# Every fourth plain-product PSUM tile moves from a pool of six banks to a pool of two

## The chip, the cores and the metric

The kernel runs on one core of one Trainium2 chip. The metric is the device time of one execution in microseconds (us); the time of a kernel is the median of several executions. A core has a matrix engine (TensorE, PE in the profile), a vector engine (VectorE, DVE), an activation engine (ScalarE, ACT), GpSimd (POOL) and SyncE (SP), which here only issues transfers (DMA). TensorE writes its products into PSUM, which this program uses as eight banks of 128 x 512 fp32; VectorE and ScalarE read them out. Weight loads of TensorE have their own row, PEld.

## The reference

With x of 2048 rows and 1024 columns, all inputs bf16, the reference computes two branches and mixes them by a gate per row:

```
g  = sigmoid((x * gate_w).sum(-1))
a  = attention(x @ wqkv) @ wo            # 32 heads of 32; each row sees 8 keys, 2 rows apart, backwards
z  = gelu(x @ w_in)                      # 3584 columns
z1 = z[:, :1792];  z2 = layernorm(z[:, 1792:])
b  = (z1 * (w_sp @ z2 + b_sp)) @ w_out   # w_sp is 2048 x 2048
out = g * a + (1 - g) * b
```

## The kernel before

The program is written out flat, and each engine runs its instructions in the order in which they were written. Some work is placed by a planner (class `Beat`, L237): it keeps a clock that advances with the columns that TensorE has been given (`beat.run`), and emits small jobs (loads, norms, pieces of the attention on VectorE) when they are due by that clock.

TensorE's work comes in stages. First come the products for z2 and for q, k, v, interleaved: `z2_block` (L307, matmuls on L312) and `qkv_tile` (L602, matmuls on L607), 64 and 128 tiles. Then comes the z1 stage (L700 to L718): 64 tiles, numbered 0 to 63 below, each of 8 matmuls of 448 columns (L710), evacuated by ScalarE with a gelu (L712) into one of two staging slots of four tiles, `z1s_slots`, which SP stores to DRAM after every fourth tile (L717). Then comes the mixing stage: 16 groups (`g_group`, L752) of seven products of 8 matmuls each (L725), a Strassen-like scheme for w_sp @ z2. Then comes the product with wo (L877 to L886, 32 tiles `psa`), and the last stage (L900 to L935), eight blocks of seven products with w_out. z1, the mixing and the last stage need VectorE to prepare sums of operands (`s_sums`, L487; `t_sums`, L496; `y_sums`, `w_sums`), and VectorE also does the whole attention between the z2 stage and the end of the mixing.

PSUM is divided in two pools (L82, L83): `psum` with six banks and `seeded` with two. Within a pool a tile takes the bank that has been free longest; its first matmul waits until the bank's last reader is done. Before the change the plain products (z2, qkv, z1, wo) and the `pa`, `pd` tiles of the mixing and last stage all take banks of `psum`. The banks of `seeded` serve the warm-up (L105) and `fork` (L744): there ScalarE copies a half-done sum from a `psum` bank into a `seeded` bank, and TensorE goes on adding to that copy.

Three other jobs lie inside the z1 stage. `row_store` (L465), due 20 us after its beginning by the planner's clock, takes a `psum` bank `pt` for two small transposes (L467, L468), which VectorE reads with two small instructions (L469, L470) that stand in VectorE's queue behind attention and layernorm work; the store to `rs_d` that follows (L474) waits for VectorE, and the stores and loads issued after it wait behind it on SP. `squares` (L668, L671) and `w_norm` (L542, L543) are ScalarE passes over 1792 columns each, ten and eight of them in this stage; `w_norm` reads pieces of w_out that SP loads into two slots (L540). `w_power` (L550) takes one more `psum` bank before the last four tiles, read by VectorE (L553).

In a group of the mixing, `fork` (L749), `keep` (L735, L737), the copy of `pb` (L767) and the last piece (L776) are ScalarE's; two additions (L741) and the product with z1 (L777) are VectorE's. `scale_rows` (L485) and `s_sums` (L489, L490) for the next pair of groups stand in VectorE's queue after the first group of the pair before.

Of the kernel before, what the change touches and what calls it, by code (L numbers as in the profile page):

```python
# [10 lines left out]
F32 = mybir.dt.float32  # L11
# [4 lines left out]
P = 128  # L16
# [40 lines left out]
def _sub_ap(t, offset_elems, dims):  # L57
    return bass.AP(tensor=t.tensor, offset=t.offset + offset_elems, ap=[list(t.ap[0])] + [list(d) for d in dims])
# [3 lines left out]
def kernel(  # L62
# [19 lines left out]
    psum = ctx.enter_context(tc.tile_pool(name="psum", bufs=6, space=bass.MemoryType.PSUM))  # L82
    seeded = ctx.enter_context(tc.tile_pool(name="seeded", bufs=2, space=bass.MemoryType.PSUM))  # L83
# [4 lines left out]
    def reg(off, n):  # L88
        return arena[:, off:off + n]
# [6 lines left out]
    rs_d = dpool.tile([S], BF, name="rs_d")  # L96
    wop_d = dpool.tile([D, D], BF, name="wop_d")
    o_d = dpool.tile([S, D], BF, name="o_d")

    warm = reg(R_OFF + 35200, 512)  # L100
    nc.vector.memset(warm, 0.0)
# [180 lines left out]
    def v_order(g):  # L282
        wgt = wg_slots[g % 3]
        vdst = wgt[:, 2, :, :].rearrange("p k (d h) -> p k d h", d=DH, h=HG)
        vsrc = wgt[:, 3, :, :].rearrange("p k (h d) -> p k d h", h=HG, d=DH)
        nc.scalar.copy(vdst, vsrc)
# [17 lines left out]
    def z2_tile(i, c):  # L304
        z2_block([(i, c)])

    def z2_block(blocks):  # L307
        banks = [psum.tile([P, 512], F32, name="ps", tag="ps") for _ in blocks]
        for kt in range(KT):
            for ps, (i, c) in zip(banks, blocks):  # L310
                N = ZC + 1 if c == 3 else ZC
                nc.tensor.matmul(ps[:, 0:N], xT[:, kt, i * P:(i + 1) * P], w2[:, kt, ZC * c:ZC * c + N],  # L312
                                 start=(kt == 0), stop=(kt == KT - 1))
        for ps, (i, c) in zip(banks, blocks):
            z2_out(ps, i, c)

    def z2_out(ps, i, c):
        nc.scalar.activation(z2[:, i, ZC * c:ZC * (c + 1)], ps[:, 0:ZC], ACT.Gelu_apprx_tanh,  # L318
                             accum_out=s1[:, 4 * i + c:4 * i + c + 1])
        if c == 3:  # L320
            nc.scalar.copy(gl_s[:, i:i + 1], ps[:, ZC:ZC + 1])
        beat.run(KT * ZC)
# [199 lines left out]
    def load_w1(c):  # L522
        sync.dma_start(w1_slots[c], win_v[:, :, ZC * c:ZC * (c + 1)])
# [32 lines left out]
    def load_rows_y(u):  # L556
        for r in range(2):
            sync.dma_start_transpose(rows[u % 5].whole[r], y_d[(2 * u + r) * P:(2 * u + r + 1) * P, :])
# [42 lines left out]

    def qkv_tile(g, j):  # L602
        wgt = wg_slots[g % 3]
        ps = psum.tile([P, 512], F32, name="ps", tag="ps")
        for kt in range(KT):
            lhsT = xT[:, kt, j * P:(j + 1) * P] if g == 0 else _sub_ap(xT_flat, kt * S + j, [[NJ, P]])
            nc.tensor.matmul(ps[:, 0:3 * C].rearrange("p (t c) -> p t c", t=3), lhsT, wgt[:, 0:3, kt, :],  # L607
                             start=(kt == 0), stop=(kt == KT - 1))
        st = stage_slots[stg[0] % 3]
        if g == 0:  # L610
            nc.scalar.copy(st[:, j % 4, 0:2 * C], ps[:, 0:2 * C])
            nc.scalar.copy(st[:, j % 4, 2 * C:3 * C].rearrange("p (d h) -> p d h", h=HG),
                           ps[:, 2 * C:3 * C].rearrange("p (h d) -> p d h", h=HG))
        else:
            nc.scalar.copy(st[:, j % 4, :], ps[:, 0:3 * C])  # L615
        if j % 4 == 3:
            row, step, first = (C, P * C, (j - 3) * P) if g == 0 else (NJ * C, C, j - 3)
            for n, (t_d, off) in enumerate(((q_d, g * S), (k_d, g * (S + 16) + 16), (v_d, g * (S + 16) + 16))):
                sync.dma_start(bass.AP(tensor=t_d.tensor, offset=t_d.offset + (off + first) * C,
                                       ap=[[row, P], [step, 4], [1, C]]), st[:, :, n * C:(n + 1) * C])  # L620
            stg[0] += 1
        if j == 8 and g + 1 < NG:
            v_order(g + 1)
        projected[g] += 1
        beat.run(KT * 3 * C)

    warm_up(6)
    xpose(0, 2)
    z2_block([(i, c) for c in range(2) for i in range(2)])
    for i in range(2, 8):  # L630
        z2_tile(i, 0)
    beat.steps = vector_steps(beat.now + NJ * KT * 3 * C * BEAT + 8.0)
    for j in range(NJ):
        qkv_tile(0, j)
# [11 lines left out]
    for g in range(1, NG):  # L646
        if g + 1 < NG:
            load_wg(g + 1)
        for j in range(NJ):
            qkv_tile(g, j)  # L650
        if g == 1:
            for i in range(8, 16):
                z2_tile(i, 0)
# [14 lines left out]
    def squares():  # L668
        i = square[0]
        square[0] += 1  # L670
        nc.scalar.activation(junk[:, 0:FH], z2[:, i, :], ACT.Square, accum_out=s2[:, i:i + 1])  # L671
        if i % 4 == 3:
            beat.at(beat.now + 4.0, lambda i=i: stats(i))
            for ii in range(i - 3, i + 1):
                beat.at(beat.now + 8.0, lambda ii=ii: norm(ii))
# [24 lines left out]
    for c in range(4):  # L700
        w1 = w1_slots[c]
        if c == 0:
            load_w1(2)
        for i in range(16):
            if c == 2 and i == 6:
                load_w1(3)
            z1s = z1s_slots[(i // 4) % 2]
            ps = psum.tile([P, 512], F32, name="ps", tag="ps")
            for kt in range(KT):
                nc.tensor.matmul(ps[:, 0:ZC], xT[:, kt, i * P:(i + 1) * P], w1[:, kt, :],  # L710
                                 start=(kt == 0), stop=(kt == KT - 1))
            nc.scalar.activation(z1s[:, i % 4, :], ps[:, 0:ZC], ACT.Gelu_apprx_tanh)  # L712
            beat.run(KT * ZC)
            if square[0] < 16 and i % 3 == 2:
                squares()
            if i % 4 == 3:
                sync.dma_start(bass.AP(tensor=z1_d.tensor, offset=z1_d.offset + (i - 3) * P * FH + (2 * (c % 2) + c // 2) * ZC,  # L717
                                       ap=[[FH, P], [P * FH, 4], [1, ZC]]), z1s)  # L718
# [158 lines left out]
    for a in range(16):  # L877
        if a == 12:
            beat.at(beat.now + 0.5, lambda: load_rows_y(2))
        for c in range(2):  # L880
            psa = psum.tile([P, 512], F32, name="psa", tag="ps")
            for kt in range(KT):
                nc.tensor.matmul(psa[:], oT[a][:, kt, :], wo_sb[:, kt, 512 * c:512 * (c + 1)],  # L883
                                 start=(kt == 0), stop=(kt == KT - 1))
            nc.scalar.activation(mix[a][:, 512 * c:512 * (c + 1)], psa[:], ACT.Copy, scale=g_s[:, a:a + 1])  # L885
            beat.run(KT * 512)  # L886
# [79 lines left out]
```

## Time and profile before

| | |
|---|---|
| median of 3 runs | 690.04 us (689.43 to 690.09) |
| profiled execution | 689.91 us, of which the span from first to last instruction is 688.1 us |
| mean granted TensorE clock over the span | 0.997 |
| TensorE busy | 677.1 us |
| VectorE, ScalarE busy | 514.2 us, 367.0 us |
| z1 stage | 270.96 to 375.3 us |
| mixing | 375.3 to 544.8 us |
| product with wo | 544.8 to 600.05 us |
| last stage's matmuls | 600.05 to 684.7 us |

Times in the profile are microseconds from the span's start unless marked ns. A line of the timeline gives start, length, engine, source line, operation, tile written and read, shape and count, and in brackets the engine's idle time before it and what ended that. A line of the waits gives who waited for whom: total us, times, longest. A line of the windows gives the busy time of each engine in a stretch, then the granted clock of TensorE as a share of full speed, then the share of the DMA engines' time and GB/s.

### The profile page before, as it was taken

To read this page: it belongs to the slowest core of one execution; us is meant where nothing else is said; L and a number is where in the kernel's file an instruction comes from. 1 tells how busy PE (TensorE), PEld (TensorE's weight loads), DVE (VectorE), ACT (ScalarE), POOL (GpSimd) and SP (SyncE) were. 2 spreads that over 40 slices of the span, in tenths; PEclk is the share of its full clock that TensorE was granted. 3 is DMA by queue.
4 is the path that set the end of the run, shared out by engine and by line. 5 is a ranking of instruction groups with operands and counts; after the bars stand their busy time and mean duration, and the time that the engine had idled before them with its cause. 6 is when DMAs were issued, how large, how long until landed. Compare 5 with 4: busy or idle time off the path is not lost.

```text
span 688.1 us, 9397 instructions
## 1 busy us (share of the span) xinstructions
PE 677.1 (98%) x3618; PEld 395.6 (57%) x3618; DVE 514.2 (75%) x554; ACT 367.0 (53%) x690; POOL 13.1 (2%) x23
## 2 busy tenths in 40 slices
PE   8999999999999999989899999999999999999997
PEld 4577788888875555545445555555555444444443
DVE  0009799999999999999999999999936338035645
ACT  4345666565545886838853456455455553422221
POOL 1000000000000000012100000000000000000000
PEclk9999999999999999999999999999999999999999
DMA  8999779999759751446935735485579999055311
GB/s 223 178 222 234 215 184 268 230 266 217 200 136 266 274 171 59 163 106 201 299 109 164 177 93 145 116 236 151 130 217 246 232 289 202 21 117 127 73 62 61
DMA packets 229148, 121.80 MB, mean 177 GB/s; under 512 B 190832, under 2 KB 215664, under 8 KB 229104
## 3 DMA queue, kind: packets, MB, share of 16 engines
q1 hardware_dynamic: 229104, 121.21, 67.5%
q8 instruction: 28, 0.46, 0.3%
q14 instruction: 16, 0.13, 0.1%
HBM read 61.87 MB, written 37.82 MB: 145 GB/s over the span
## 4 chain that ended last, share of the span: by engine, by line
PE 84%; DVE 6%; ACT 3%; DMA 3%; SPq 2%; issue 1%; ACTq 0%; DVEq 0%
PE ps L725 32%; PE ps L607 24%; PE ps L312 10%; PE psa L883 8%; PE seed L725 5%; PE ps L710 5%; DMA z_d<-arena 2%; SPq L592 1%; DVE arena L368 1%; ACT arena L671 1%; ACT arena L712 1%; ACT arena L543 1%; DVE arena L338 1%; DVE arena L512 1%; DMA arena<-in_A_wqkv_dram 1%; DVE arena L335 1%
## 5 line engine op out<-in xcount | busy, mean ns | idle before, releaser
L725 PE MATMUL ps<-arena 128*128 128x448 f16 (+1 forms) x1104 | 222.0, 361 | 0.0
L725 PEld LDWEIGHTS <-arena 128*128 128x128 f16 x1288 | 126.0, 98 | 128.1
L607 PE MATMUL ps<-arena 128*128 128x384 bf16 x1024 | 166.7, 326 | 0.9 <-DMA arena<-in_A_wqkv_dram 0.9
L607 PEld LDWEIGHTS <-arena 128*128 128x128 bf16 x1024 | 141.6, 138 | 26.0 <-issue 1.3
L335 DVE TENSOR_TENSOR arena<-arena 128x8192 bf16<-128x8192 bf16 x16 | 70.7, 4420 | 46.9 <-DMA arena<-k_d 46.7
L710 PE MATMUL ps<-arena 128*128 128x448 bf16 x512 | 99.2, 356 | 4.9 <-ACT arena L712 2.7
L312 PE MATMUL ps<-arena 128*128 128x448 bf16 (+1 forms) x512 | 97.6, 353 | 0.1
L615 ACT CAST arena<-ps 128x384 bf16<-128x384 f32 x112 | 51.5, 483 | 59.6 <-PE ps L607 54.4
L710 PEld LDWEIGHTS <-arena 128*128 128x128 bf16 x512 | 50.4, 99 | 53.0 <-issue 7.4
L338 DVE TENSOR_TENSOR arena<-arena 128x4096 bf16<-128x4096 bf16 (+1 forms) x64 | 77.6, 1212 | 2.0
L312 PEld LDWEIGHTS <-arena 128*128 128x128 bf16 x512 | 50.0, 98 | 46.8 <-issue 0.4
L368 DVE TENSOR_TENSOR arena<-arena,att_A 128x8192 bf16<-128x8192 bf16 x16 | 70.7, 4422 | 0.2
L883 PE MATMUL psa<-arena 128*128 128x512 bf16 x256 | 55.4, 379 | 0.0
L318 ACT ACTIVATE arena<-ps 128x448 bf16<-128x448 f32 x64 | 34.7, 547 | 31.2 <-PE ps L312 30.5
L712 ACT ACTIVATE arena<-ps 128x448 bf16<-128x448 f32 x64 | 33.4, 560 | 33.7 <-PE ps L710 25.7
L898 DVE SCALAR_TENSOR_TENSOR arena<-seed,omr,arena 128x512 bf16<-128x512 f32 x8 | 6.0, 751 | 56.2 <-PE seed L725 56.2
L883 PEld LDWEIGHTS <-arena 128*128 128x128 bf16 x256 | 25.0, 98 | 30.2
L725 PE MATMUL seed<-arena 128*128 128x448 f16 (+1 forms) x184 | 40.2, 361 | 0.0
L885 ACT ACTIVATE arena<-psa,g_s 128x512 f32<-128x512 f32 x32 | 22.0, 686 | 31.4 <-PE psa L883 31.4
L374 DVE TENSOR_TENSOR arena<-arena 128x4096 bf16<-128x4096 bf16 x16 | 36.6, 2290 | 0.4
L737 ACT ACTIVATE arena<-ps,bt 128x448 f32<-128x448 f32 x32 | 20.3, 633 | 29.5 <-PE ps L725 27.5
L894 ACT ACTIVATE arena<-ps,omr 128x512 f32<-128x512 f32 x24 | 16.5, 687 | 32.8 <-PE ps L725 32.8
(109 smaller groups left out, 509.8 us busy)
## 6 DMA issues: line engine op xcount, KB each, us to landing
arena<-in_B_w_sp_dram SPq DMA_DIRECT2D x16, 512.0 KB, 5.1
arena<-k_d SPq DMA_DIRECT2D x8, 960.0 KB, 7.8
arena<-v_d SPq DMA_DIRECT2D x8, 960.0 KB, 6.0
z_d<-arena SPq DMA_DIRECT2D x16, 448.0 KB, 2.7
arena<-z_d SPq DMA_DIRECT2D x16, 448.0 KB, 3.7
y_d<-arena SPq DMA_DIRECT2D x16, 448.0 KB, 3.3
arena<-in_A_wqkv_dram SPq DMA_DIRECT2D x24, 256.0 KB, 5.4
arena<-in_B_w_in_dram SPq DMA_DIRECT2D x6, 896.0 KB, 7.8
```

What stands on the lines that cost most here:

```text
L312: nc.tensor.matmul(ps[:, 0:N], xT[:, kt, i * P:(i + 1) * P], w2[:, kt, ZC * c:ZC * c + N], start=(kt == 0), stop=(kt == KT - 1))
L318: nc.scalar.activation(z2[:, i, ZC * c:ZC * (c + 1)], ps[:, 0:ZC], ACT.Gelu_apprx_tanh, accum_out=s1[:, 4 * i + c:4 * i + c + 1])
L335: TT(prod.rearrange("p (w j c) -> p w j c", w=W, j=8, c=C), in0, in1, ALU.mult)
L338: return lambda: TT(pv[:, :, 0:half], pv[:, :, 0:half], pv[:, :, half:2 * half], ALU.add)
L368: TT(prod.rearrange("p (w j d h) -> p w j d h", w=W, j=8, d=DH, h=HG), in0, in1, ALU.mult)
L374: return [(4.4, mul), (2.3, lambda: TT(p3[:, 0:4, :], p3[:, 0:4, :], p3[:, 4:8, :], ALU.add)), (1.2, lambda: TT(p3[:, 0:2, :], p3[:, 0:2, ...
L607: nc.tensor.matmul(ps[:, 0:3 * C].rearrange("p (t c) -> p t c", t=3), lhsT, wgt[:, 0:3, kt, :], start=(kt == 0), stop=(kt == KT - 1))
L615: nc.scalar.copy(st[:, j % 4, :], ps[:, 0:3 * C])
L710: nc.tensor.matmul(ps[:, 0:ZC], xT[:, kt, i * P:(i + 1) * P], w1[:, kt, :], start=(kt == 0), stop=(kt == KT - 1))
L712: nc.scalar.activation(z1s[:, i % 4, :], ps[:, 0:ZC], ACT.Gelu_apprx_tanh)
L725: nc.tensor.matmul(ps[:, 0:c1 - c0], w[:, k, :], v[:, k, c0:c1], start=(first and k == 0), stop=(k == K - 1), skip_group_check=True)
L883: nc.tensor.matmul(psa[:], oT[a][:, kt, :], wo_sb[:, kt, 512 * c:512 * (c + 1)], start=(kt == 0), stop=(kt == KT - 1))
```

## The change

A counter is added, and a function `bank()` that takes every fourth tile it is asked for from `seeded` (under the tag that `fork` uses) and the other three from `psum`. The four plain products take their tiles from it: `z2_block`, `qkv_tile`, the z1 loop and the wo loop. `pa`, `pd`, `pt`, the bank of `w_power` and `fork` are as before. The sizes of the pools, the instructions and their order are unchanged.

```diff
+    taken = [0]
+
+    def bank():
+        taken[0] += 1
+        pool, tag = (seeded, "sd") if taken[0] % 4 == 0 else (psum, "ps")
+        return pool.tile([P, 512], F32, name=tag, tag=tag)
...
     def z2_block(blocks):
-        banks = [psum.tile([P, 512], F32, name="ps", tag="ps") for _ in blocks]
+        banks = [bank() for _ in blocks]
...
     def qkv_tile(g, j):
         wgt = wg_slots[g % 3]
-        ps = psum.tile([P, 512], F32, name="ps", tag="ps")
+        ps = bank()
...
             z1s = z1s_slots[(i // 4) % 2]
-            ps = psum.tile([P, 512], F32, name="ps", tag="ps")
+            ps = bank()
...
         for c in range(2):
-            psa = psum.tile([P, 512], F32, name="psa", tag="ps")
+            psa = bank()
```

## The prediction

> **What bounds the kernel now.** I read the page's busy line first, then TensorE's waits, then the timelines of TensorE, ScalarE and VectorE around those waits, then the granted clock there, and last VectorE in the mixing, where an earlier TensorE would arrive.
>
> ```profile
> PE 677.1 (98%) x3618; PEld 395.6 (57%) x3618; DVE 514.2 (75%) x554; ACT 367.0 (53%) x690; POOL 13.1 (2%) x23
> ```
>
> TensorE works for 677.1 of 688.1 us; with its instructions unchanged, only its 11 us of idle time and slow clock can give. Its waits, all of them over 0.4 us:
>
> ```profile
> PE ps L710 <- ACT arena L712: 2.7, 1, 2.7
> PE ps L710 <- DVE bt L470: 2.2, 1, 2.2
> PE pw L107 <- DVE arena L101: 1.2, 1, 1.2
> PE ps L607 <- DMA arena<-in_A_wqkv_dram: 0.9, 1, 0.9
> ```
>
> The last two wait for inputs at the start. The first two are waits of a z1 tile for a PSUM bank, once each. No wait of this kind stands in z2, qkv, the wo product, the mixing or the last stage. Where they fall, in TensorE's timeline:
>
> ```profile
> 292.50 6.23 PE L710 MATMUL ps<-arena 128*128 128x448 bf16 x32
> ...
> 300.96 39.51 PE L710 MATMUL ps<-arena 128*128 128x448 bf16 x208 [2.23 <-DVE bt L470]
> 343.17 26.06 PE L710 MATMUL ps<-arena 128*128 128x448 bf16 x128 [2.70 <-ACT arena L712]
> 369.06 0.17 PE L552 MATMUL ps<-wl_n,zeros 128*128 128x1 bf16 x1
> ```
>
> At 8 matmuls per tile, 14 tiles run before the transposes into `pt` at 292.24, then 4 tiles (14 to 17), a stop at 298.73, 26 tiles (18 to 43), a stop at 340.47, 16 tiles (44 to 59), and `w_power`. The second stop has a cost beyond itself, in the windows:
>
> ```profile
> 298.00:300.00 2.00, 0.73 (x4) 0.29 (x3) 2.00 (x5) 0.54 (x1) 0.00 (x0) 1.00 0.00 0
> ...
> 301.00:302.00 1.00, 1.00 (x6) 0.54 (x6) 0.97 (x3) 0.00 (x0) 0.00 (x0) 1.00 0.02 4
> ...
> 344.00:345.00 1.00, 1.00 (x4) 0.43 (x3) 0.96 (x2) 1.00 (x1) 0.00 (x0) 0.50 0.63 225
> ...
> 347.00:348.00 1.00, 1.00 (x7) 0.52 (x6) 1.00 (x2) 1.00 (x1) 0.00 (x0) 1.00 0.07 26
> ```
>
> After 2.23 us of idle time the granted clock is 1.00; after 2.70 us it is 0.50 (0.66 in the microsecond before and 0.64 from 346 to 347), and 1.00 again from 347. What ScalarE did meanwhile:
>
> ```profile
> 304.79 0.53 ACT L712 ACTIVATE arena<-ps 128x448 bf16<-128x448 f32 x1
> ...
> 312.10 0.98 ACT L712 ACTIVATE arena<-ps 128x448 bf16<-128x448 f32 x2 [6.78 <-DMA z_d<-arena]
> ...
> 339.47 1.70 ACT L543 ACTIVATE arena<-arena 128x1792 bf16<-128x1792 bf16 x1 [2.43 <-DMA arena<-in_B_w_out_dram]
> ...
> 342.57 1.42 ACT L712 ACTIVATE arena<-ps 128x448 bf16<-128x448 f32 x3
> ```
>
> ScalarE stops after tile 19 for a staging slot whose store (L717) was held on SP behind L474 and L481; from 312.10 it never waits for TensorE, works off a backlog with squares and w_norm passes between, waits 2.43 us for a piece of w_out, and reaches tile 38 at 342.57. TensorE stood at tile 44, which takes tile 38's bank: 44 - 38 = 6 banks.
>
> **The change part by part.** No instruction, operand or transfer is added or removed and no queue's order changes, so no DMA or issue is to be charged on SP or POOL. Each first matmul of a tile still waits for one earlier reader; only which reader changes.
>
> z2, qkv (192 tiles) and wo (32): TensorE has no bank wait there, so eight banks instead of six gain 0; they cost 0, as ScalarE reads all these tiles in order, wherever they lie. 192 is a multiple of 4, so z1 tile k lies in `seeded` where k mod 4 is 3.
>
> First stop. `pt` lies in a bank that comes up again behind four others. Tiles 15 and 19 now take `seeded` banks, so 14, 16, 17 and 18 use up the four, and tile 20 meets `pt`'s bank, two tiles later than tile 18 did. One tile takes 1.515 us (ScalarE's L712 starts at 351.16 and 375.40, 16 tiles apart). TensorE arrives at 298.73 + 2 x 1.515 = 301.76. VectorE's L470 ends at 300.75 + 0.15 = 300.90, and its queue does not depend on TensorE here. The stop of 2.23 us goes, with 0.8 us to spare.
>
> Second stop. ScalarE's times from 312.10 on hang on SP's store at 306.83, which stands behind L474 and VectorE's small instructions at 301, and not on TensorE; so tile 38 is still read out at 343.1. What is late next is ScalarE itself. With eight banks tile 46 waits for it instead of 44. TensorE gets there at 298.73 + 28 x 1.515 + 0.12 (the same tail as at 340.47) = 341.27 and stops for 343.17 - 341.27 = 1.90 us. In between nothing binds: tile 28, the first to meet the late bank of tile 20, is due at 313.9 and ScalarE frees that at 312.6. So at 343.17 TensorE starts tile 46 where it had started tile 44: 2 x 1.515 = 3.03 us gained, however the 4.93 us of the two stops were split.
>
> Clock. From 343.17 to `w_power` at 369.06 there are 25.89 us for 16 tiles; at 1.515 they need 24.24, so the slow stretch cost 1.65. The stop that is left, 1.90 us, is shorter than the 2.23 that was followed by 1.00; I take 0 for it, as that row is the nearest (0.33 us away, against 0.80 to the 2.70). The bounds are 0 and 1.65. The sum is 3.03 + 1.65 = 4.68 us at `w_power`, 364.4 instead of 369.06. [...]
>
> Behind it, does the lead last? The mixing begins at 370.6 instead of 375.3. TensorE does not wait for VectorE there now, but VectorE is not moved by the change:
>
> ```profile
> 377.38 4.93 DVE L338 TENSOR_TENSOR arena<-arena 128x4096 bf16<-128x4096 bf16 x4
> ...
> 383.57 0.62 DVE L741 TENSOR_TENSOR arena<-arena 128x448 bf16<-128x448 f32 x1 [1.26 <-ACT arena L737]
> ...
> 390.51 2.34 DVE L485 TENSOR_TENSOR arena<-arena,rs_b 128x2048 f16<-128x2048 bf16 x2
> 392.88 1.29 DVE L489 TENSOR_TENSOR arena<-arena 128x1024 f16<-128x1024 f16 x2
> 394.10 1.41 DVE L490 TENSOR_TENSOR arena<-arena 128x1024 f16<-128x1024 f16 x2
> ```
>
> VectorE is busy up to 382.31; of the 4.68 it takes only its 1.26 us of idle time. A group takes 10.59 us (7 x 1.513). Group 2, the first that needs fresh sums, began at 375.30 + 21.18 = 396.48 and would begin at 391.80. Its first operand (half of L485) is ready at 391.7 - 1.26 = 390.4, the first sum (half of L489) at 393.5 - 1.26 = 392.3 for the product at 393.3, the next (half of L490) at 394.8 - 1.26 = 393.5 for 394.8. So 1.0 us is the tightest spare, and the cover is enough; were VectorE not to move at all, 0.3 us would be missing at the second product, and the stop would be 0.3. Later VectorE gains on TensorE through its idle times before L741 and L777, in which it waits for ScalarE or TensorE (0.61, 0.46, 0.22, 0.22, 0.96, 0.57, 0.42), which with the 1.26 make 4.72 by 471 us. The nearest other place is group 6: `g_ring` is rewritten at 444.95, which would be 440.3; the store of the old content is issued at 439.81 less 2.77 (the first five idle times), 437.0, and with 2.7 us to landing (the median of these stores from 400 to 460) frees it at 439.7. Should it land 1 us later, ScalarE's L767 would wait as it does once now (1.98 us, at 530.8) without a wait of TensorE. From there the end of the attention, the loads of wo and w_out and the last stage follow TensorE by queues, and keep the lead.
>
> So the profiled 689.91 us (1.8 around the span of 688.1) become 685.2; the median of the runs lies 0.13 above the profiled one, 690.04 - 4.68 = 685.4. I take 685.3, the middle.
>
> **The rivals.** *The clock drops again* after the stop of 1.90 us. For it: the boundary between 2.23 and 2.70 rests on one stop each, and where the stop falls against whatever the chip counts is not shown; against it: 1.90 is the shortest of the three. The gain is 3.03: 687.0. [...] *The lead is lost in the mixing*: sums, a store or a w_sp load come late, and TensorE waits for what VectorE finishes at its old time. For it: only 1.0 us to spare at group 2; against it: by the rows at most 0.3 us is missing there. A wait that takes a quarter to the half of the lead gives 686.5 to 687.7; one that takes it all gives 690.0, the change that does nothing. *Slower*: TensorE meets group 2's second product with the sums still missing and stands there until it has given back the whole lead; idle for 4.68 us, it would be slowed after it as at 343.17, for 1.65 us, so 691.7. It decides if the first sum ends at 398.0 or later, where it now ends at 393.5; a w_sp load 4.5 us later than now would do that, and nothing that the change moves delays that load, which starts after the last z1 tile and so earlier. *That the change doesn't reach the stop* (the bank of tile 38 met again at 44) would be 690.0; the count of six between 38 and 44 speaks against it.
>
> **How the numbers follow.** A measurement of this kernel can tell about 0.2% (1.4 us) from no change. Forecast 685.3 (684.6 to 686.1): 0.78. Clock drops again, 687.0: 0.09. Part of the lead lost, 686.5 to 687.7: 0.04. All lost or not reached, about 690.0: 0.05. Slower, 691.7: 0.04. So faster 0.91, same 0.05, slower 0.04. The range 684.6 to 687.2 takes in the first two cases and half the third, which leaves out about 0.11; the likeliest alone is 684.6 to 686.1.
>
> **What would show it.** Right: in TensorE's waits the line on `bt` L470 is gone and one line on L712 of about 1.9 us stays, with ScalarE's start after the table load still near 342.6; the granted clock is 1.00 from 343 to 347; `w_power`'s matmul is near 364.4 and the first mixing matmul near 370.6; no wait of L725. Wrong: 0.50 after 343 (687.0); a wait of L725 or of its weight load for VectorE between 391 and 396; ScalarE reaching tile 38 at another time than 342.6, since everything before 343 hangs on that.

## The result and the profile after

The changed kernel takes 685.07 us (median; 683.77 to 688.53), the kernel before 689.52 us in the same comparison. The ratio is 0.9944, with a 95% interval of 0.9918 to 0.9969. The forecast of 685.3 and its range hold. The nine executions of the changed kernel lie in two groups, five from 683.77 to 685.07 and four from 686.99 to 688.53; the profiled one is of the upper group (688.53 us, span 686.8), so its profile shows both the gain and what takes part of it back. The mean granted clock is 0.997 or 0.998 in each of the four and 0.999 or 1.000 in the five.

Seven lines are new near the head of the file, so each line number from there on is higher by 7 than before: z1 is L717 with ScalarE's read L719, the mixing L732 with L744, the wo product L890. Where an experiment adds a line of its own, the numbers behind it rise by as many again. The busy line of the page, then all TensorE waits over 0.6 us:

```profile
PE 676.4 (98%) x3612; PEld 395.3 (58%) x3618; DVE 513.3 (75%) x554; ACT 366.8 (53%) x690; POOL 13.2 (2%) x23
```

```profile
PE ps L732 <- ACT arena L744: 2.2, 1, 2.2
PE ps L717 <- ACT arena L719: 1.8, 1, 1.8
PE pw L114 <- DVE arena L108: 1.2, 1, 1.2
PE ps L614 <- DMA arena<-in_A_wqkv_dram: 1.0, 1, 1.0
```

The wait on `bt` is gone, the wait on L719 has become 1.8 us, and a wait in the mixing is new. TensorE's timeline, as before with start, length, line and, in brackets, the idle time and what ended it:

```profile
337.52 3.19 PE L717 MATMUL ps<-arena 128*128 128x448 bf16 x16
342.52 1.67 PE L717 MATMUL ps<-arena 128*128 128x448 bf16 x8 [1.81 <-ACT arena L719]
...
363.70 0.17 PE L559 MATMUL ps<-wl_n,zeros 128*128 128x1 bf16 x1
...
369.78 4.70 PE L732 MATMUL ps<-arena 128*128 128x448 f16 x24
...
524.14 3.19 PE L732 MATMUL ps<-arena 128*128 128x448 f16 x16
529.49 7.90 PE L732 MATMUL ps<-arena 128*128 128x448 f16 x32 [2.16 <-ACT arena L744]
...
543.28 1.89 PE L890 MATMUL ps<-arena 128*128 128x512 bf16 x7
```

`w_power` stands at 363.70 instead of 369.06, a lead of 5.36 us. It is 0.68 more than the 4.68 forecast, nearly all of it because ScalarE came to tile 38 earlier, so that the stop ended at 342.52 and not at 343.17. The mixing's first matmul is at 369.78 instead of 375.14, and the lead is whole until 524. At the last product of group 14 (of 0 to 15) TensorE stops for 2.16 us, and the wo product begins at 543.28 instead of 544.63: 1.35 us of 5.36 are left, which is what the span gained (688.1 to 686.8). The granted clock behind the two stops, in the windows (the figure before the last two of each line):

```profile
343.00:344.00 1.00, 1.00 (x7) 0.49 (x5) 1.00 (x3) 1.00 (x2) 0.00 (x0) 1.00 0.81 322
344.00:345.00 1.00, 1.00 (x8) 0.51 (x6) 0.96 (x3) 1.00 (x3) 0.00 (x0) 1.00 1.09 384
...
530.00:531.00 1.00, 1.00 (x5) 0.44 (x3) 0.63 (x2) 0.97 (x3) 0.00 (x0) 0.50 1.33 209
...
533.00:534.00 1.00, 1.00 (x5) 0.44 (x4) 1.00 (x2) 0.00 (x0) 0.00 (x0) 0.80 1.25 271
```

After 1.81 us it stays at 1.00; after 2.16 us it is 0.50 from 530 to 533 and 0.80 from 533 to 534. The 32 matmuls that took 7.90 us there take 6.21 in the run below whose clock stays up, so the loss is 2.16 + 1.69 = 3.85 us. Between the five and the four executions lie 3.4 us (medians 684.56 and 687.96).

What ScalarE did ahead of the stop in group 14, first in the kernel before, then in the changed one:

```profile
528.19 0.63 ACT L737 ACTIVATE arena<-ps,bt 128x448 f32<-128x448 f32 x1 [0.98 <-PE ps L725]
530.80 0.53 ACT L767 CAST arena<-seed 128x448 bf16<-128x448 f32 x1 [1.98 <-DMA y_d<-arena]
531.23 0.64 ACT L737 ACTIVATE arena<-ps,bt 128x448 f32<-128x448 f32 x1
```

```profile
522.83 0.63 ACT L744 ACTIVATE arena<-ps,bt 128x448 f32<-128x448 f32 x1 [0.98 <-PE ps L732]
528.37 0.53 ACT L774 CAST arena<-seed 128x448 bf16<-128x448 f32 x1 [4.91 <-DMA y_d<-arena]
528.80 0.64 ACT L744 ACTIVATE arena<-ps,bt 128x448 f32<-128x448 f32 x1
```

ScalarE wants to overwrite a buffer of `y` whose store is not done. Its wait has grown from 1.98 to 4.91 us, because TensorE's products come 5.36 us earlier and the store only 2.43. The `keep` behind it (L744) frees the PSUM bank that TensorE needs. In the kernel before, that bank was free at 531.23 + 0.64 = 531.87, and TensorE, without a stop, came to it at 529.50 + 2 x 1.513 = 532.53: 0.66 us of cover. So 5.36 - 2.43 - 0.66 = 2.27 us had to be waited, and 2.16 were. With seven banks (below), where TensorE came here 2.12 us and ScalarE's copy 1.00 us earlier than in the kernel before, the same sum gives 0.46, and 0.51 was stood.

Why the store moved by only 2.43 us, in SP's own timeline of before and after (the transfer's line, its count, how long SP stood at it):

```profile
502.30 0.57 SPq L389 DMA_DIRECT2D o_d<-arena  x1
507.91 0.37 SPq L443 DMA_DIRECT2D arena<-wop_d  x1
508.38 9.99 SPq L478 DMA_TRANSPOSE arena<-in_B_w_sp_dram  x2
...
527.54 1.03 SPq L533 DMA_DIRECT2D y_d<-arena  x2
```

```profile
496.94 0.57 SPq L396 DMA_DIRECT2D o_d<-arena  x1
502.96 0.37 SPq L450 DMA_DIRECT2D arena<-wop_d  x1
503.43 10.41 SPq L485 DMA_TRANSPOSE arena<-in_B_w_sp_dram  x2
...
523.15 1.03 SPq L540 DMA_DIRECT2D y_d<-arena  x2
```

In VectorE's timeline after, its wait for the w_sp rows and the scaling of y that stands behind them:

```profile
514.35 1.23 DVE L492 TENSOR_TENSOR arena<-arena,rs_b 128x2048 f16<-128x2048 bf16 x1 [4.90 <-DMA arena<-in_B_w_sp_dram]
...
520.94 1.54 DVE L584 TENSOR_SCALAR arena<-arena,ys 128x896 f16<-128x896 bf16 x4
```

The w_sp rows start 4.95 us earlier (508.38 to 503.43), VectorE's scaling of y, which stands behind them in VectorE's queue, 4.72 us (525.66 to 520.94), the issue of the store 4.39 (527.54 to 523.15). From that issue to ScalarE's restart it took 3.26 us before (527.54 to 530.80) and 5.22 after (523.15 to 528.37); 1.96 of the 2.93 us by which this chain fell behind TensorE (5.36 - 2.43) lie in this last step.

### The profile page after: what moved, and what is told of

Same layout as the page of the kernel before. It is cut to its first block, busy times and chain, and to the rows that moved or that the text cites. A ratio compares the mean times of both kernels' runs of the same rounds, so it can differ in the third digit from the quotient of the medians.

```text
span 686.8 us, 9395 instructions
## 1 busy us (share of the span) xinstructions
PE 676.4 (98%) x3612; PEld 395.3 (58%) x3618; DVE 513.3 (75%) x554; ACT 366.8 (53%) x690; POOL 13.2 (2%) x23
## 4 chain that ended last, share of the span: by engine, by line
PE 92%; DMA 3%; ACT 2%; SPq 2%; issue 0%; DVE 0%; ACTq 0%
PE ps L732 32%; PE ps L614 18%; PE ps L319 9%; PE ps L717 8%; PE sd L614 6%; PE ps L890 6%; PE seed L732 5%; PE sd L319 3%; PE sd L717 3%; PE sd L890 2%; SPq L599 1%; DMA z_d<-arena 1%; DMA arena<-in_A_wqkv_dram 1%; DMA y_d<-arena 1%; ACT arena L719 1%; ACT arena L550 1%
## 5 line engine op out<-in xcount | busy, mean ns | idle before, releaser
L732 PE MATMUL ps<-arena 128*128 128x448 f16 (+1 forms) x1104 | 223.9, 362 | 2.2 <-ACT arena L744 2.2
L732 PEld LDWEIGHTS <-arena 128*128 128x128 f16 x1288 | 126.5, 98 | 131.6 <-issue 4.5
L614 PE MATMUL ps<-arena 128*128 128x384 bf16 x768 | 130.3, 326 | 1.0 <-DMA arena<-in_A_wqkv_dram 1.0
L717 PEld LDWEIGHTS <-arena 128*128 128x128 bf16 x512 | 49.9, 98 | 48.5 <-issue 2.1
L717 PE MATMUL ps<-arena 128*128 128x448 bf16 x384 | 75.6, 352 | 1.8 <-ACT arena L719 1.8
L319 PE MATMUL ps<-arena 128*128 128x448 bf16 (+1 forms) x384 | 76.8, 353 | 0.5 <-DMA arena<-in_B_w_in_dram 0.5
L622 ACT CAST arena<-ps 128x384 bf16<-128x384 f32 x84 | 39.5, 484 | 45.0 <-PE ps L614 41.9
L614 PE MATMUL sd<-arena 128*128 128x384 bf16 x256 | 46.8, 326 | 0.0
L890 PE MATMUL ps<-arena 128*128 128x512 bf16 x187 | 42.3, 379 | 0.2
L890 PEld LDWEIGHTS <-arena 128*128 128x128 bf16 x256 | 25.0, 98 | 30.2
L732 PE MATMUL seed<-arena 128*128 128x448 f16 (+1 forms) x184 | 40.2, 361 | 0.0
L325 ACT ACTIVATE arena<-ps 128x448 bf16<-128x448 f32 x48 | 26.1, 548 | 24.5 <-PE ps L319 23.9
L719 ACT ACTIVATE arena<-ps 128x448 bf16<-128x448 f32 x48 | 25.5, 570 | 25.4 <-PE ps L717 25.3
L744 ACT ACTIVATE arena<-ps,bt 128x448 f32<-128x448 f32 x32 | 20.3, 634 | 29.5 <-PE ps L732 29.4
```

The lines of the kernel that those rows point to most:

```text
L732: nc.tensor.matmul(ps[:, 0:c1 - c0], w[:, k, :], v[:, k, c0:c1], start=(first and k == 0), stop=(k == K - 1), skip_group_check=True)
```

## The experiments

Each was timed in five rounds beside the kernel before on the same chip; the second time given below is the median of that kernel in the same comparison.

**Where the gain is made: z1 or the other products.** Two complementary kernels. The first keeps `bank()` in z1 and wo only, the second everywhere but in z1.

```diff
 # z1 and wo only, against the changed kernel
-        banks = [bank() for _ in blocks]
+        banks = [psum.tile([P, 512], F32, name="ps", tag="ps") for _ in blocks]
...
-        ps = bank()          # in qkv_tile
+        ps = psum.tile([P, 512], F32, name="ps", tag="ps")
```

```diff
 # all but z1, against the changed kernel
-            ps = bank()      # in the z1 loop
+            ps = psum.tile([P, 512], F32, name="ps", tag="ps")
```

> Only z1 and wo take every fourth tile from the pool of two; z2 and qkv stay on six banks. Theory (all of the gain is made in z1): as the changed kernel. One wait of a z1 tile for L712's evacuation of tile 38 of 1.8 to 1.9 us, none for VectorE's read of pt, granted clock 1.00 after it, first mixing matmul near 370. Whole time 684.5 where group 14 of the mixing does not wait, about 688 where it does. Rival (z2 and qkv share in the gain): slower than the changed kernel by the share that they have, so between 685 and 689.5, with the first z1 matmul later than 270.7 us.

> z2, qkv and wo take every fourth tile from the pool of two; z1 stays on six banks. Theory: as the kernel before, 689.5 us, with both z1 waits (2.2 us for VectorE's read of pt, 2.7 us for L712) and the clock at 0.50 after the second. Rival (the other stages share in the gain): below 688.5.

z1 and wo only: 685.15 us (683.16 to 690.71) against 689.98, ratio 0.9935 (0.9907 to 0.9963). All but z1: 690.36 against 689.98, ratio 0.999 (0.9966 to 1.0014). Timeline of TensorE, all but z1:

```profile
300.47 41.06 PE L717 MATMUL ps<-arena 128*128 128x448 bf16 x208 [2.28 <-DVE bt L477]
343.68 26.06 PE L717 MATMUL ps<-arena 128*128 128x448 bf16 x128 [2.15 <-ACT arena L719]
```

With six banks in z1 both stops are back (4.43 us together), whatever the other stages use. The gain is z1's, and z2, qkv and wo are worth nothing that can be told, as forecast. After both of these stops the clock was low (behind the first the 208 matmuls took 41.06 us, against 39.51 in the kernel before; behind the second it was 0.50 from 345 to 348), although the second is shorter than the 2.23 us behind which the prediction had seen the clock stay up. In the profile of z1 and wo only (684.88 us) the z1 stop lasted 1.19 us, where 1.8 to 1.9 had been expected, and group 14 stopped for 1.50, with the clock at 1.00 behind both. So an execution near the forecast time can stop in group 14 too. Five of its twelve executions lie over 686.5.

**One stop without the other.** z2, qkv and z1 keep six banks (z1's last two tiles take the others, so that the mixing finds its banks free), but the small transposes take a `seeded` bank, so nothing in z1 waits for VectorE. The lines that put z2 and qkv back on `psum` are left out here, as they stand above.

```diff
-        pt = psum.tile([P, 4, P], BF, name="pt", tag="ps")
+        pt = seeded.tile([P, 4, P], BF, name="pt", tag="sd")
...
-            ps = bank()      # in the z1 loop
+            pool, tag = (seeded, "sd") if 16 * c + i >= 62 else (psum, "ps")
+            ps = pool.tile([P, 512], F32, name=tag, tag=tag)
```

> z1 keeps six banks, but row_store's pt takes a bank of the pool of two, so that no z1 tile meets it (the last two z1 tiles and every fourth wo tile take that pool too, after both stops). Theory (TensorE's place after the second stop is fixed by ScalarE's evacuation of tile 38 at about 342.6 and by the number of banks, however the idle time was split): the wait for pt is gone, the wait for L712 grows from 2.7 to about 4.9 us at the same end, 343.2, the clock falls to 0.50 after it, and the whole time is that of the kernel before, 689.5 us (689.0 to 690.2). Rival (the two stops are independent costs): 2.2 us faster, 687.3.

690.18 us against 689.98, ratio 0.9994 (0.9968 to 1.0019): no gain. TensorE's timeline:

```profile
313.78 27.40 PE L718 MATMUL ps<-arena 128*128 128x448 bf16 x144 [1.83 <-ACT arena L720]
344.49 25.85 PE L718 MATMUL ps<-arena 128*128 128x448 bf16 x128 [3.31 <-ACT arena L720]
```

The stop on VectorE is gone and its time is stood at other places: 1.83 us at tile 26, which meets the bank of tile 20 (the one that ScalarE holds back for its staging slot), and 3.31 us at tile 44, 5.14 in all where the two of before had 4.93. ScalarE came to tile 38 1.3 us later here (343.89 against 342.57), so the last stop also ended later. A single longer stop had been expected; it split in two. The sum is what counts: with six banks, tile 44 starts when ScalarE frees the bank of tile 38, and a wait taken away before it is waited there.

**Seven banks.** Every seventh z1 tile takes a `seeded` bank; z2 and qkv keep six (again not shown).

```diff
-            ps = bank()      # in the z1 loop
+            pool, tag = (seeded, "sd") if (16 * c + i) % 7 == 6 else (psum, "ps")
+            ps = pool.tile([P, 512], F32, name=tag, tag=tag)
```

> z1 rotates over seven banks instead of eight (every seventh tile from the pool of two), wo as in the changed kernel, z2 and qkv on six. Theory: one tile of lead instead of two. pt's bank is met at tile 19, a first stop of 0.7 us; the second stop is before tile 45, about 2.7 us, ends at 343.2 and is followed by 0.50 as in the kernel before; so the gain is 1.5 us, 688.0. If the clock stays at 1.00 after it, 686.4. Rival (the gain is not a matter of tiles of depth, but of the pt wait alone): 2.2 us or more faster, 687.3 or below with the clock at 0.50.

689.35 us against 689.98, ratio 0.998 (0.9954 to 1.0006): no difference that can be told. The profile says more:

```profile
300.77 1.67 PE L718 MATMUL ps<-arena 128*128 128x448 bf16 x8 [0.71 <-DVE bt L477]
...
344.08 4.70 PE L718 MATMUL ps<-arena 128*128 128x448 bf16 x24 [3.80 <-ACT arena L720]
```

```profile
345.00:346.00 1.00, 1.00 (x7) 0.52 (x6) 1.00 (x2) 1.00 (x1) 0.00 (x0) 1.00 0.68 243
```

One bank takes 1.5 us off the first stop (2.23 to 0.71), as one tile's time would, and `w_power` comes at 366.78. Here ScalarE was 0.9 us late (a piece of w_out), so the last stop ended at 344.08 and not at 343.17. The stop of 3.80 us, the longest idle time in z1 of any run here, was followed by a clock of 1.00.

**What holds ScalarE back in z1.** In the kernel before, with its six banks, only the store to `rs_d`, on which SP stood while the z1 store waited behind it, is issued 6 us later, and the load behind it too.

```diff
-        sync.dma_start(rs_d.rearrange("(a t) -> a t", t=P), rs_r[:])
+        beat.at(beat.now + 6.0, lambda: sync.dma_start(rs_d.rearrange("(a t) -> a t", t=P), rs_r[:]))
...
-    beat.at(t + 22.0, lambda: load_scale(0))
+    beat.at(t + 28.0, lambda: load_scale(0))
```

> The kernel before, six banks everywhere, with the store of rs (and the load that reads it back) put 6 us later into SP's queue, so that the z1 stores issued meanwhile do not stand behind it. Theory (the second stop of z1 is the backlog that ScalarE gets from the z1 store held on SP): ScalarE's wait of 6.8 us for a staging slot falls below 2, the second stop is gone, the first, 2.2 us for VectorE's read of pt, stays and may still be followed by 0.50 for 3.4 us in some executions. 689.98 - 2.7 = 687.3, or 685.6 where the clock had been 0.50 after the second stop alone. Rival (the second stop comes from w_norm's wait for its pieces of w_out at 337 us): the stop stays and the time is that of the kernel before.

686.51 us against 690.17, ratio 0.9948 (0.9927 to 0.997). TensorE's timeline:

```profile
300.40 63.72 PE L710 MATMUL ps<-arena 128*128 128x448 bf16 x336 [2.30 <-DVE bt L470]
363.96 0.17 PE L552 MATMUL ps<-wl_n,zeros 128*128 128x1 bf16 x1
```

The second stop is gone without a single bank more, and `w_power` stands at 363.96, within 0.3 us of the changed kernel. ScalarE's wait for a staging slot (6.78 us before) is gone too, while its wait for the piece of w_out is still there:

```profile
335.36 1.70 ACT L543 ACTIVATE arena<-arena 128x1792 bf16<-128x1792 bf16 x1 [1.95 <-DMA arena<-in_B_w_out_dram]
```

So that wait alone makes no stop, and the rival fails: without the z1 store held on SP, ScalarE frees the bank in time. But in the kernel before the two delays add up. Without the 2.43 us for w_out ScalarE would have reached tile 38 at 342.57 - 2.43 = 340.14, by estimate, and TensorE, there at 340.47, would have stopped for about 0.3 us instead of 2.70. This run too stopped in group 14 (2.06 us, then 0.50), so that wait comes with the lead and not with the banks.

**The same with eight banks.** The edit of the last experiment in the changed kernel.

> The changed kernel with the same later store of rs. Theory: no stop in z1 is left, the first mixing matmul comes 1.9 us earlier than in the changed kernel, at about 368; VectorE's sums for group 2 are not moved, so a wait of up to 1 us for VectorE appears before group 2's second product; group 14's wait for the y store may stay. 683.5 where it does not, 686 to 687 where it does. Rival (the lead that is gained so is all lost again behind VectorE in groups 2 to 6): as the changed kernel, 685.1.

685.23 us against 690.17, ratio 0.9931 (0.9908 to 0.9954): no better than the change alone. z1 now has no stop, and the mixing begins at 368.20, 6.9 us earlier than before the change (375.14), but:

```profile
390.39 1.69 PE L732 MATMUL ps<-arena 128*128 128x448 f16 x8 [0.84 <-DVE arena L492]
392.26 3.20 PE L732 MATMUL ps<-arena 128*128 128x448 f16 x16 [0.17 <-DVE arena L496]
...
529.01 6.21 PE L732 MATMUL ps<-arena 128*128 128x448 f16 x32 [1.90 <-ACT arena L744]
```

Group 2 now meets VectorE's sums before they are ready, and 1.01 us of the lead go there. The prediction had 1.0 us of cover at a lead of 4.7; at a lead of 6.9 it would be short by 1.3, and 1.01 was stood. The stop in group 14 is there again, at 1.90 us and with the clock at 1.00 after it; it is this line that the 7.90 us of the changed kernel were set against.

**The wait in group 14.** In the changed kernel VectorE scales y (`y_scale`) behind the w_sp rows of the next pair. Here, at the one pair in which these rows come behind the load of wo, y is scaled and its store queued first.

```diff
-        if fb == 0 and u > 0:
+        if fb == 0 and u == 6:
+            y_power(u - 1)
+            y_scale(u - 1)
+            soon(("y", u - 1), lambda u=u: y_done(u - 1))
+        elif fb == 0 and u > 0:
             y_finish(u - 1)
```

> The changed kernel, with one step moved: after group 12 VectorE scales y of block 5 before it scales the w_sp rows of block 7, which it waits for, instead of after. Theory (the new wait of the mixing, 2.16 us in the changed kernel's profile and 1.50 in the z1-and-wo version, is ScalarE's wait in group 14 for the store of y of block 5, which stands behind VectorE's wait for the w_sp rows): the store is issued about 8 us earlier, ScalarE's copy of pb in group 14 does not wait, no wait of the mixing products, and the granted clock is 1.00 in nearly every execution, since the z1 wait left is under 2 us. Median near 684.3, highest under 686.5. Rival (the wait hangs on something else than the order on VectorE): the wait stays and the executions stay between 683.8 and 688.5.

684.12 us (683.44 to 685.15) against 690.17, ratio 0.9915 (0.9891 to 0.9939), the lowest median, level with the next experiment's. SP, ScalarE and TensorE at this place:

```profile
517.38 1.04 SPq L540 DMA_DIRECT2D y_d<-arena  x2
```

```profile
523.98 0.53 ACT L774 CAST arena<-seed 128x448 bf16<-128x448 f32 x1 [0.88 <-PE seed L732]
```

```profile
523.78 9.24 PE L732 MATMUL ps<-arena 128*128 128x448 f16 x48
...
538.91 5.34 PE L894 MATMUL ps<-arena 128*128 128x512 bf16 x23
```

The store is issued 5.8 us earlier (523.15 to 517.38), ScalarE does not wait for it, TensorE runs through, and the wo product begins at 538.91: 4.37 us earlier than in the profiled execution of the changed kernel, whose time lies 4.34 higher (688.53 to 684.19). z1 is as in the changed kernel, with one stop of 1.72 us. None of the six executions lies in the upper group. Set against the changed kernel (ratio 0.9944, 0.9918 to 0.9969) the two intervals overlap: that the step ends the stop is shown, how much it takes off the median is not.

**Both edits.** y first and the store to `rs_d` later, with eight banks.

> The changed kernel with both: the later store of rs and y of block 5 scaled before the w_sp rows of block 7. Theory: neither the z1 stop nor group 14's wait; median near 683, granted clock 1.00 in nearly all executions, and the narrowest spread of the four. Rival: a wait for VectorE in groups 2 to 6 takes what the later store gave, and it equals the version with the y step alone.

684.19 us (683.55 to 684.99) against 690.17, ratio 0.9916 (0.9892 to 0.994). With no stop in z1 and none in group 14 it equals y first alone: TensorE stops for 0.89 and 0.18 us in group 2, and that gives back what the 1.72 us in z1 were worth, to 0.3 us at the wo product (539.18 against 538.91). From the later store with eight banks it differs by the y step alone: 684.19 against 685.23, and four executions over 685.5 there (of eight), none here (of six).

**y first without the banks.** The y step in the kernel before.

> The kernel before, six banks everywhere, with the y step of the version that scales y of block 5 before the w_sp rows of block 7. It asks whether group 14's wait came with the change or was there before it. Theory (it was there in some executions before: ScalarE waited 1.98 us for the y store in the profile of before, a little less than stops TensorE, and the lead moves that place as a whole): the time is 0.3 to 1.5 us below the kernel before, and its highest executions (693 and more) are gone. Rival (the wait is new, brought by the lead): the same as the kernel before, 690, with executions above 693 as often.

689.04 us against 689.45, ratio 0.999 (0.9971 to 1.001): no difference that can be told, so the 0.3 to 1.5 us of the theory are not shown. Its two stops in z1 are 2.25 and 2.93 us. The step that ends a stop in the changed kernel gains nothing that can be told where TensorE has no lead to lose. (None of the 12 executions is over 690.7 while the kernel before has some up to 694; whether the wait in group 14 exists there now and then was not seen in a profile.)

**Getting past group 2.** To y first and the later store is added that VectorE does the row scaling and the sums for the second pair before the product of group 0.

```diff
         nc.scalar.activation(g[:, 1, 0], pa[:, 0:ZC], ACT.Identity, bias=hi)
+        if n == 0:
+            for h in range(2):
+                scale_rows(1, h)
+            for fn in s_sums(1):
+                fn()
+            beat.on_vector(5.3)
         TT(g, g, z, ALU.mult)
...
-        if fb == 0 and u + 1 < NU:
+        if fb == 0 and 0 < u < NU - 1:
```

The last two lines take this work away from its old place behind group 0.

> The version with both steps (later store of rs, y of block 5 first), and in group 0 VectorE makes the sums for group 2 before its product with z1 instead of after it. Theory (the lead that the later store gains is held back at group 2 by VectorE, 0.89 and 0.18 us of waits in that version's profile): the sums are ready 1.0 us earlier, at most 0.3 us of wait is left at group 2, and the time falls by 0.8 us, to about 683.4. Rival (the lead is held back further on as well): the wait at group 2 goes, another for VectorE appears in groups 4 to 6, and the time stays at 684.2.

689.06 us against 689.79, ratio 0.9997 (0.9978 to 1.0016): a miss, for the theory (683.4) and for the rival (684.2). The waits of TensorE and ScalarE:

```profile
PE ps L732 <- ACT seed L756: 4.4, 1, 4.4
...
PE ps L732 <- DVE arena L496: 0.2, 1, 0.2
```

```profile
ACT arena L570 <- DVE arena L790: 7.0, 1, 7.0
```

The wait for the sums shrank to 0.17 us. But ScalarE's norm of y (L570) takes the delayed product, waited 7.0 us for it, and the `fork` that stands behind it in ScalarE's queue held TensorE for 4.41 us, with a slow clock after it (eight matmuls in 2.95 us, where the eight before the stop took 1.69). So this move of VectorE's work does not widen the lead; other orders were not tried.

**The wo load out of the way.** The changed kernel, with the load of wo issued later, so that the w_sp rows follow the store of the attention's output at once.

```diff
-        load_wo()
+        beat.at(beat.now + 18.0, load_wo)
```

> The changed kernel with one load moved: wo (2 MB) is loaded after the store of y of block 5 instead of before the w_sp rows of block 7. Theory (the w_sp rows of block 7 are late because they stand on SP behind the wo load's wait of 5.4 us for the last attention store and then share the transfer engines with its 2 MB): the rows are issued about 6 us earlier, VectorE's wait of 4.9 us for them is gone, the y store is issued earlier and group 14 does not wait: 684.3, as in the version with the y step. The wo load lands before the wo product begins. Rival (the rows are late for another reason): VectorE's wait for them stays over 3 us and group 14 waits in some executions, 685 to 688.5.

684.77 us against 689.45, ratio 0.9925 (0.99 to 0.995). SP's timeline, then TensorE's in z1 and the windows behind that:

```profile
499.72 0.57 SPq L396 DMA_DIRECT2D o_d<-arena  x1
500.38 7.31 SPq L485 DMA_TRANSPOSE arena<-in_B_w_sp_dram  x2
...
518.56 1.10 SPq L540 DMA_DIRECT2D y_d<-arena  x2
```

```profile
343.62 2.98 PE L717 MATMUL ps<-arena 128*128 128x448 bf16 x8 [1.98 <-ACT arena L719]
```

```profile
344.00:345.00 1.00, 1.00 (x4) 0.40 (x3) 1.00 (x2) 1.00 (x3) 0.00 (x0) 0.50 0.68 272
...
347.00:348.00 1.00, 1.00 (x6) 0.49 (x5) 1.00 (x2) 1.00 (x2) 0.00 (x0) 0.89 0.00 0
```

The rows are no longer issued behind the wo load (0.66 us after the o store's issue, not 6.49), and ScalarE's copy in group 14 no longer waits for the store of y, only for TensorE:

```profile
527.12 0.53 ACT L774 CAST arena<-seed 128x448 bf16<-128x448 f32 x1 [0.88 <-PE seed L732]
```

This is a second, independent way to have the store in time. That TensorE has no stop in group 14 says less here than with y first, as its lead there was only 2.6 us (the wo product begins at 542.05), and by the sum above so small a lead would hardly have met a stop there in any case. The profiled execution took 687.3 us because the stop in z1, 1.98 us long, ended 1.1 us later than in the changed kernel and was followed by half clock. Three of its eight executions are over 686, each with a mean granted clock of 0.997 or 0.998 where the others have 0.999 or 1.000, so the rival that the clock drops again does occur.

## Why the prediction was right, and where it was not

*First stop.* Right. It is gone; one tile more of distance took 1.5 us off it (seven banks), two took all.

*Second stop.* Right in the mechanism, with some luck in the number. Forecast 1.90 us, measured 1.81, with tile 46 beginning where 44 did (342.52 against 343.17, ScalarE being 0.65 earlier, mostly by a shorter wait for the piece of w_out: 1.90 against 2.43). TensorE, too, came 0.56 earlier than forecast (340.71 against 341.27), mostly because z1 began 0.40 earlier (270.56), and the two shifts nearly cancel in the length. The prediction took ScalarE's time at tile 38 as fixed. In the nine profiles whose kernels leave SP's queue in z1 as it was, the last z1 stop ends anywhere from 341.21 to 344.49, and in the four of them with eight banks it is 1.19 to 1.98 us long. That the split of the 4.93 us does not matter, only the last stop's end and the number of banks, is shown by the run without the first stop (nothing gained) and by the all-but-z1 run. That the z1 store held on SP is what made ScalarE late enough, with the wait for w_out on top, is shown by the later store.

*Other products.* Right at 0.

*Clock.* The outcome was right, the reason only half. The prediction argued by length: 1.90 is shorter than a 2.23 that kept the clock. Behind 1.98, 2.06, 2.15 and 2.16 us the clock fell, behind 2.23, 2.30 and 3.80 it stayed up. So length alone does not decide. The rival's price (687.0) fits the one execution that shows it, 687.3 in the last experiment.

*Cover in group 2.* Right. VectorE's row scaling, forecast at 390.51 - 1.26 = 389.25, began at 388.77, its first sum at 391.18, and TensorE did not wait. The two runs with a lead of 6.9 us show that the cover ends where the prediction put it, to 0.3 us. (Were VectorE not to move at all, its own rows give 393.5 - 393.3 = 0.2 us missing, not 0.3.)

*"From there the end of the attention, the loads of wo and w_out and the last stage follow TensorE by queues, and keep the lead."* Wrong, and this is the step that failed. The prediction had named ScalarE's 1.98 us wait for the store of y at 530.8, and passed over it because no TensorE wait went with it. It did not work out the cover, which its own profile gave: 0.66 us. The w_sp rows did follow the attention (5.0 us earlier), but the store's last step did not, and the wait behind it took 2.16 us and then the clock. In the profiled execution 3.85 of 5.36 us went there. y first ends this stop. The later wo load, which acts on another engine's queue, ends ScalarE's wait for the store as well, but only with y first did all executions stay together.

*The rivals.* "The lead is lost in the mixing" was near the size (686.5 to 687.7 forecast; of the four executions at 686.99 to 688.53, two are above that), and it named a late store among the causes, but it looked for the loss in group 2, and it came in group 14. Its chance of 0.04 was too low. All four show a clock that fell once, by their mean of 0.997 or 0.998 (the profiles with one slow stretch have such a mean, the one with two has 0.995); only the profiled one is shown to owe it to group 14, and in the others it may have been the stop in z1. That the median met the forecast is partly luck: 685.07 is the slowest of the five executions that lost no clock, and with one more in the upper group the median would have been near 687. What those five stood in group 14 was not seen, as none of them has a profile. *Slower* and *the change doesn't reach the stop* did not come.

## What to carry to other kernels

A stop taken away on a saturated engine is worth only what the last stop behind it lets through (the first stop alone, taken away, was worth nothing that can be told: 690.18 us against 689.98), so compute the end of the last one and count the buffers up to it. Then follow the lead to each later place where the idle side already waits: a wait of another engine that costs nothing today has a cover in microseconds that can be read from the same timeline (0.66 here), and a lead larger than that cover (5.36, of which the store followed by 2.43) turns it into a stop (2.16). Here, putting a short job with a store behind it ahead of a long wait on VectorE ended the stop that took back part of the banks' gain.

## What the runs showed of the hardware

**The clock after a stop.** The granted clock stayed at 1.00, by the windows, by the time of the matmuls behind the stop or by the mean of the run, behind idle times of 0.71, 1.19, 1.50, 1.72, 1.81, 1.83, 1.90, 2.23, 2.25, 2.30 and 3.80 us. It fell to 0.50 behind 1.98, 2.06, 2.15, 2.16, 2.70, 2.93 and 3.31. Behind 2.28 us the next 208 matmuls took 41.06 us, where they took 39.51 behind 2.23; behind 4.41 us the next eight took 2.95, where the eight before took 1.69. If the clock is either 1.00 or 0.50 at each moment, the windows make the slow stretch 3.40 us long in the kernel before (0.66, 0.50, 0.50 and 0.64 from 343 to 347), 3.42 in the changed kernel (0.99, three times 0.50 and 0.80 from 529 to 534) and 3.40 in the last experiment (0.91, three times 0.50 and 0.89 from 343 to 348). It cost 1.65 us in the kernel before and 1.69 in the changed one, where all of it lies behind the stop. At nearly the same idle time (2.15 and 2.28 against 2.23 and 2.25) both outcomes occur, and what decides between them is not shown by these runs.

**The store of y.** From its first issue to ScalarE's restart it took 3.26 us in the kernel before. It took 3.11 to 3.58 in the three other profiles whose mixing began at most 2.3 us earlier than in the kernel before and in which ScalarE waited for it (all but z1, one stop without the other, seven banks). It took longer in the four whose mixing began 5 us or more earlier: 5.22 in the changed kernel, 4.72 with the later store and six banks, 4.65 with eight, 4.62 with z1 and wo only. Why it is longer when the whole stage runs earlier was not settled.
